# A fused attention and Mish block on one core: a new issue order, new buffers, and the first FFN's bias loaded in rows

## The chip, the cores and the metric

The kernel runs on one core of one Trainium2 chip. The metric is the device time of one execution in microseconds (us). A core has five instruction engines, each with a queue that it works off strictly in order: PE (TensorE, matrix products; PEld is its weight load), DVE (VectorE), ACT (ScalarE), POOL (GpSimd) and SP (SyncE, which here issues DMAs). An instruction waits in its queue for semaphores that other engines or DMAs set, and everything behind it on that engine waits with it.

## The reference

The block normalises x (2048 tokens of 512 numbers), runs a linear attention and a Mish network over it, and gates the one with the other. In outline:

```python
xn = layernorm(x)                                   # S, D = 2048, 512
qkv = xn @ wqkv                                     # 32 heads of 16
phi(u) = concat(softmax(u @ w_phi), softmax(-(u @ w_phi)))      # of each head, for q and k
kv, z = phi_k^T v, sum(phi_k)
s = (phi_q kv / (phi_q z + 1e-6)) @ wo
h = xn @ w1 + b1                                    # F = 1792
g = silu((h * tanh(softplus(h))) @ w2)
out = x + s * g
```

All is float32.

## The kernel before

The tokens lie in 16 tiles of 128 on the partitions. Every operand of a product is split into a part hi and a rest lo, and one product of float32 is three passes of TensorE (`mm3`: lo x hi, hi x lo, hi x hi). ACT writes hi, DVE or POOL writes lo = source - hi.

At the start, the weights of k and q are multiplied by `w_phi` on TensorE: `folded` makes one fold (`wkf`, `wqf`), and `wkh`, `wkl`, `wqh`, `wql` are its two parts. There are four folds for k and four for q. Meanwhile `norm(t)` loads a tile of x; takes its statistics (DVE alone for tiles 0, 1, 4 and 5; for the others ACT, in two passes into a scratch tile `dev`, with sums in `st` and `mv`); POOL takes the power -1/2 (`rs`); DVE makes `nb`; one instruction scales x in place; TensorE transposes it into a PSUM bank (`pt`), and `xT` receives the two parts of the transpose. Tiles go in pairs t and t + 4: `sums_x` copies the second transpose (`xr`) and makes four sums and differences of the two (`ts`), so that pairs of tiles and pairs of weight blocks need seven products where eight would do otherwise (the weights' sums are `ws`). Tiles 0 and 4 are also multiplied in the plain way (`k_0`, `v_0`, `v_4`). Results of k go through two softmaxes (`k0m` is the maximum and minimum of each head, `k0e` the differences to them), and `zacc` adds them up. q is written to DRAM and read again later. Then come the attention sums, the first FFN in the same seven-product manner (`fx`, `fz`, `fy`), the second FFN with the Mish at its load (`load_m`, which adds the bias `b1t`), and the output tile by tile (`final`): Silu, times s, plus x, store.

No engine's order is left to a scheduler. The parts are built in the order of a table `ORDER`, but building only records: every operation is put into a list by the class `Program`. Where an operation may run on either of two engines (`either`: DVE or POOL; `copy`: DVE or ACT; the scaling of x likewise), both forms are recorded. At the end, `issue()` goes through the text table `SCHED`: a number is an operation, and a letter behind it (V, G, A for DVE, POOL, ACT) picks an engine other than the first recorded. The order of `SCHED` is thus the order of every engine's queue at once, and since all instructions are issued by one line, they all show as L184 in the profile. All DMAs are issued by SP, except the first in the list, which goes to ACT's queue; eight hardware lanes take them in turn (`DMAHW0` to `DMAHW7`).

The second table, `PLACE`, gives the buffer of each tile in the order in which tiles are asked for: a bank of PSUM (eight), a slot of 4 KB (`slot`), a slot of 2 KB (`s2`), and so on. Two tiles with the same buffer are ordered by semaphores: the later one's first write waits for the last read of the earlier one.

The first 11 products of `wake`, on a tile of ones, use nothing that is loaded, and stand ahead of the folds.

In the rows of the issue order, names carry the number of the tile's allocation. `x_152`, `pt_158`, `xT_156` belong to tile 0; `x_180`, `pt_186`, `xT_184` to tile 1; `x_164`, `pt_170`, `xT_168`, `xr_171`, `ts_172` to tile 4; `x_216`, `pt_222`, `xT_220` to tile 5; `x_227`, `x_252`, `x_241`, `x_280`, `x_371` to others. `wkf_162` and `wkf_161` are folds of the first half of k's weights, `wkf_179` and `wkf_178` of the second; `v_215` is the value product of tile 0, `v_273` of tile 4, `q_238` and `q_279` the q of tiles 0 and 1, `q_207` and `q_250` of tiles 4 and 5.

Of the kernel before, what the change touches and what calls it, by code (L numbers as in the profile page):

```python
# [50 lines left out]
179V 410 158 237 189 411 62 286 61G 141V 180 238V 241 226 319 239 242 243 137 244 197 124 117 287 217 445 245 142 246
190V 583 412 185 181 63 338 288 321 320 247 82 107 167 123V 143 168 165A 198 218 182 267 219 339 199V 303 340 186A
248V 144V 169A 341 170 249 413 108V 200 253A 125 289V 250 109G 201 254 255V 204A 227 257 446 202 322 203 233 396 145
323 251 324 621 110 331V 256G 373 229 183 187 205 216 325 230 207V 414 447 90 397 220 268G 415 342 206V 262 234V 399
398 208 228A 449 146 290 263 161 450 111 451 294A 162G 315 221A 112 448 304V 332 222 305 264A 316V 343 416A 91 265
333G 166 126A 364 252 297V 223 306 258 235 295 224 374 260 259G 296V 344 269 231A 400 298 375 317 291 365A 307 271 377
401 326V 299 378 270V 417 379 354 376 309G 272 402 380 381V 327 273 382 355 275G 334 386A 292 403A 274 113G 293 350
261 387 452 622V 418 345A 351 388V 335A 300V 328 366 352A 624V 356 346 367A 358G 336 421V 383 301 347 308 623G 209 440
384 276G 422 211 390 368 277 481 353 357 453A 389V 359G 430 348 92 310G 360 329 479 431 330 210G 311 159 432 467 480A
419 441A 482 454 468A 278 212 404 391 434G 369 433 405 483 458A 435G 370 423V 279 424G 436 406 442 93G 425 437 469 393  # L60
443V 371A 625G 349 426 494 232 470 302 361 427G 496 495A 506 497 392G 455 472 491 438 407 507 225 439G 492A 461V 312
372 394 531 508A 484 459 509 529 460G 498 511G 527 530V 485G 471 544 313 280G 510 462 541 499 545A 500G 456 532 543
542A 486G 533 362 512G 547 528A 501V 734 444 585V 385 502 473V 428 548V 487 474G 573 493 513 363V 546 463 488 517 464G
549 534 554 514 584G 673 561 518 555A 429 314V 420 613 535G 580 562 599 489 536G 556 586G 571 614V 537 515 519 516G
595 538 640 563 521G 663 520 667 564 582 465 581V 594 707 574A 490V 575 572A 475 565V 659 596 587V 566G 735 503 633
522G 597A 678 476 592G 603 567 477 523 568 557 634A 478G 664 569 558 604 539 524 570G 550 665 605 643 593V 600 671
615V 598 657 616V 588 504 551 658A 661 525 674V 505V 636 660 526V 559A 637 618V 617 716G 635 676V 620 641A 737G 619V
638A 632 601A 717G 626 662 682 466 606 666 560 675G 576 683A 577 669 589V 630V 647 578A 552A 579 709 553 700 631V 679V
668 644 672 627V 457 602 729 607V 720 639 540V 701A 685 590 608V 591V 645A 642 646 686V 670 721G 687 628 708 648 702
718G 649 684 677G 724 703V 651V 690 719V 730A 722 629V 704 609 710V 749 705 711G 610 706 742 723G 846 750A 691 650 731  # L70
743A 680 652G 745 732 725A 692 681G 653 726 611 746A 688 736 689 744 1017 772V 738G 733 851 761 693 727 612G 778 739
751 654 844 800 712 694V 752 747 695G 765 655 748 656V 696 758 848 876 766V 845 697 755 698 768 740 699G 754 773V 774
762V 775G 777 759 852 769A 843 779 788 1059 763 808 753V 855 776G 819V 820 789 713 877 767 854 786G 790V 764 791 793
821 770 787G 796 802 771 853 814 871 797 714 824 865 756A 825V 894 794A 822 801 823 872V 826 830 811 757 780 827A 803G
856 1061 728 828 804G 792 889 929 829A 781V 878 782G 868 741 835V 857G 783 873 850 805 798 784 795 907 866A 812 836
813 891 899G 964 867 869 849 884 890V 858 942 885A 900 908A 859G 837G 926 943A 860 918V 895A 981 892 785 879V 886 982A
1067 838 919 870 880G 893 955 815G 839 881 847 806 910 816G 1025 927V 901G 840G 807 951 817 920V 902 921 874 809A 818G
903 944 887 952A 882 930G 888 1008 909 932G 861 1019 933G 958 862V 841V 863G 957 831 883 953 938 922 954 842 799 931G
1110 896 923V 1109 904G 939A 1068 905G 983 945 897 864 928 999 934 984 906 956A 935G 961 940 1111 810 911 1028 898
1010G 924V 941 913G 1013 977 1018 1029 948 978A 925 1030 936 1014G 832 972 760 962 1009V 946A 985 1011V 1020V 1115  # L80
973A 875 949 1021G 1038 979 991V 1022 974 959A 1122 1012V 1004 937V 960 1040 947 986A 1005G 992 1015 987 988 833 1039A
980 966 950 993V 1031 1000V 963 1041 1002G 989 1001G 1054 912 1032A 1026A 1016V 1108 1042 1033 1117 914V 994 1069 915
1056 1003V 965 1006 1152 1034 1296 1055V 1144 995 1007G 975 1051 1035A 1123 976 1119 1057 1130 916 1058 996G 1070V
1114 1079 1124 1071G 997V 1186 1121 1080A 1052A 1081 998 1043V 1125G 1082 1036 1075 1060 917 1023 1053 1076A 967G
1083A 1084 1163 968G 1024 1145 1062G 1166 1044 1063G 1086 1100V 1116 1118 1064 1133 1131A 1101 1155G 1164A 1132 1072
834 1138 1065 990 1187A 1037 1077 1085 1169 1092G 1113 1298 1146 1136 1170A 1156 1089 1066 1137A 1102V 969 1139 1198
1093 1140 1087A 1270 1112 1103 970 1141 1120 1207 1147G 1157V 1191 1045G 1090 1148G 1046 1171 1192A 1047 1158 1048V
1126V 1049G 1188 1297 1127 1104 1159 971 1194 1199V 1105G 1160G 1073 1212 1161G 1195A 1153 1388 1172 1143 1134 1173
1149 1106G 1361 1189 1078 1142A 1050 1200 1242 1272 1190 1167 1165 1178G 1193 1824 1107 1201 1074 1088 1196 1154G 1150
1197 1204 1213V 1174 1162 1279G 1208 1210 1205 1247 1202A 1214 1219 1334G 1374 1175A 1280 1216 1506 1362 1151 1128  # L90
# [839 lines left out]
```

## Time and profile before

| what | before |
|---|---|
| device time, median of 3 runs | 489.47 us (489.24 to 489.83) |
| the profiled execution, its span | 488.0 us |
| busy, PE | 481.5 us (99%) |
| busy, DVE | 429.3 us (88%) |
| busy, ACT | 284.6 us (58%) |
| busy, POOL | 244.5 us (50%) |
| data moved | 115.55 MB, 237 GB/s |

Busy time is that of instructions that compute: waiting and issuing don't count. The profiled execution is one run of the same program with its own time, a little under the median of the others. In rows of single instructions the first number is the start in us from the span's start, the second the length; `out<-in` names the tiles with their numbers left out; a bracket at the end tells how long the engine stood idle before, and whose end released it. TensorE's products overlap a little, and a row of several lists the start of the first and the time from there to the end of the last.

### The profile page before, as it was taken

How to read it: one execution, taken by the hardware profiler on the slowest of the kernel's cores; microseconds unless marked ns; L12 is line 12 of the kernel's file. 1: busy time of each engine (PE TensorE's matmuls, PEld its weight loads, DVE VectorE, ACT ScalarE, POOL GpSimd, SP SyncE). 2: the span in 40 equal slices, each digit the busy share in tenths (PEclk: the TensorE clock that was granted, in tenths of full speed). 3: DMA queues.
4: the chain of work that ended last, by engine and by line, in shares of the span. 5: the costliest groups of instructions: out<-in, count | busy, mean ns of one | idle time of the engine just before them, and what ended most of it. 6: DMA issues, size and time to landing. Idle time of an engine off the chain costs nothing.

```text
span 488.0 us, 8581 instructions
## 1 busy us (share of the span) xinstructions
PE 481.5 (99%) x3122; PEld 397.9 (82%) x3122; DVE 429.3 (88%) x687; ACT 284.6 (58%) x447; POOL 244.5 (50%) x188
## 2 busy tenths in 40 slices
PE   9999999999999999999999999999999999999995
PEld 9888888888888888888888878888888887888884
DVE  5989898899999997999999989998678588879984
ACT  5998777235154504325434676598976677576721
POOL 2675859967335786686557963312622032412021
PEclk9999999999999999999999999999999999999999
DMA  8956649165686789879969979788486615468543
GB/s 303 346 169 233 245 173 365 69 192 198 207 289 223 234 294 303 303 213 357 333 214 283 363 242 332 239 274 279 167 262 217 230 56 163 152 210 284 168 147 140
DMA packets 65594, 115.55 MB, mean 237 GB/s; under 512 B 7056, under 2 KB 32016, under 8 KB 65552
## 3 DMA queue, kind: packets, MB, share of 16 engines
q1 hardware_dynamic: 65408, 114.98, 69.9%
q8 instruction: 24, 0.39, 0.3%
q14 instruction: 18, 0.15, 0.1%
q10 hardware_dynamic: 144, 0.03, 0.0%
HBM read 72.92 MB, written 42.07 MB: 236 GB/s over the span
## 4 chain that ended last, share of the span: by engine, by line
PE 99%; DVE 0%; ACT 0%; DVEq 0%; issue 0%; ACTq 0%
PE y L184 20%; PE fx L184 16%; PE q L184 9%; PE pw L184 9%; PE kx L184 8%; PE x L184 8%; PE fy L184 8%; PE ky L184 4%; PE fz L184 4%; PE pn L184 2%; PE kz L184 2%; PE z L184 2%; PE kvp L184 2%; PE pt L184 1%; PE v L184 1%; PE k L184 1%
## 5 line engine op out<-in xcount | busy, mean ns | idle before, releaser
L184 PE MATMUL q<-wqh,xT 128*128 128x512 f32 x128 | 42.3, 393 | 0.0
L184 ACT ACTIVATE r<-r,b1t 128x512 f32<-128x512 f32 x56 | 38.1, 719 | 1.2 <-DMA r<-hd 1.1
L184 PEld LDWEIGHTS q<-wqh,xT 128*128 128x128 f32 x128 | 24.0, 188 | 5.0
L184 PE MATMUL q<-wql,xT 128*128 128x512 f32 x64 | 24.9, 390 | 0.0
L184 ACT ACTIVATE hc<-fx 128x512 f32<-128x512 f32 x11 | 6.5, 599 | 26.8 <-PE fx L184 15.9
L184 ACT ACT_TABLE_LOAD x16 | 20.5, 1283 | 0.3
L184 POOL TENSOR_TENSOR rs<-rs,mhalf 128x1 f32<-128x1 f32 x16 | 9.7, 615 | 19.7 <-DVE rs L184 19.7
L184 DVE TENSOR_REDUCE tz<-ez 128x64 f32<-128x1024 f32 x16 | 19.2, 1206 | 0.1
L184 PE MATMUL kx<-wss,th 128*128 128x512 f32 x56 | 17.3, 390 | 0.0
L184 POOL TENSOR_TENSOR tl<-ts,th 128x1024 fp32r<-128x1024 f32 x6 | 14.4, 2407 | 4.5 <-ACT th L184 3.1
L184 DVE TENSOR_TENSOR ol<-pn,oh 128x256 fp32r<-128x256 f32 x32 | 11.9, 416 | 5.1 <-ACT oh L184 5.1
L184 POOL TENSOR_TENSOR w1al<-w1a,w1ah 128x768 fp32r<-128x768 f32 x4 | 8.2, 2046 | 14.2 <-DVE w1sl L184 9.2
L184 POOL TENSOR_TENSOR w<-w2r,w 128x512 fp32r<-128x512 f32 x7 | 9.9, 1428 | 9.3 <-ACT w L184 9.3
L184 ACT ACTIVATE qs<-q 128x512 f32<-128x512 f32 x15 | 8.7, 594 | 9.4 <-PE q L184 5.0
L184 PEld LDWEIGHTS q<-wql,xT 128*128 128x128 f32 x64 | 12.0, 188 | 2.4
L184 ACT ACTIVATE oh<-pn 128x256 fp32r<-128x256 f32 x32 | 10.7, 393 | 4.9 <-PE pn L184 3.6
L184 POOL TENSOR_TENSOR w1s<-w1a 128x256 f32<-128x256 f32 x9 | 8.9, 995 | 7.4 <-PE q L184 7.1
L184 PE MATMUL pw<-oh,wo0l 128*128 128x512 f32 x32 | 12.4, 389 | 0.0
L184 PE MATMUL pw<-ol,wo0h 128*128 128x512 f32 x32 | 12.4, 389 | 0.0
L184 PE MATMUL pw<-oh,wo0h 128*128 128x512 f32 x32 | 12.4, 389 | 0.0
L184 PE MATMUL pw<-oh,wo1l 128*128 128x512 f32 x32 | 12.4, 389 | 0.0
L184 PE MATMUL pw<-ol,wo1h 128*128 128x512 f32 x32 | 12.4, 389 | 0.0
(869 smaller groups left out, 1833.1 us busy)
## 6 DMA issues: line engine op xcount, KB each, us to landing
r<-hd SPq DMA_DIRECT2D x28, 512.0 KB, 5.0
x<-x SPq DMA_DIRECT2D x16, 256.0 KB, 6.1
scr<-xT SPq DMA_DIRECT2D x8, 512.0 KB, 5.1
scrT<-th SPq DMA_DIRECT2D x8, 512.0 KB, 3.5
qd<-qs SPq DMA_DIRECT2D x16, 256.0 KB, 4.6
scrT<-tl SPq DMA_DIRECT2D x8, 512.0 KB, 4.8
qp<-qd SPq DMA_DIRECT2D x16, 256.0 KB, 5.1
xx<-xt SPq DMA_DIRECT2D x16, 256.0 KB, 4.9
```

The costliest lines, as they stand in the source:

```text
L184: getattr(g, m)(*a, **k)
```

## The change

Two things are edited. The first is the bias of the first FFN, 1792 numbers, which is held as `b1t` with 128 partitions and 14 columns. Before, the array lies in DRAM as it comes, and the load picks for each partition 14 numbers that are 128 apart. After, the array is laid out as 128 rows of 14 before the launch, and the load takes rows.

The second is the pair of tables. The operations are the same, numbered alike; `SCHED` has a new order and for many operations another engine, and `PLACE` has other buffers.

```diff
-        Q.dma_start(b1t, b1.rearrange("(c p) -> p c", p=P))
+        Q.dma_start(b1t, b1)
...
-        "b1": np.ascontiguousarray(B_b1),
+        "b1": np.ascontiguousarray(np.asarray(B_b1).reshape(FC, P).T),
...
 SCHED = """
-11 25 0 13 1 14 2 44 3 72 4 12 17 5 94 6 26 16 7 15 27 8 28 127 29 9 10 18 36 30 31A 45 95 40 37 46 147 47 73 32 41 19
+0 1 2 3 4 5 6 25 11 7 8 9 10 12 94 96 26 27 28 29 30 16 68 31V 14 72 97 73 74 75 40 43V 98 32 41 71A 69 18 13 22 36 17
...
```

Over the whole program the list of DVE goes from 689 rows to 654, that of ACT from 424 to 408, that of POOL from 193 to 241; a row is one instruction, or several alike in a row. The list of PE has 2078 rows where it had 2076, and that of SP 322 in both.

The following rows are from the start of the program. First PE, before: from the transposes of another tile (`pt_248`) through the value products of tiles 4 and 0.

```order
L184 MATMUL pt_248<-ident,x_241 128x128 [waits DVE_49]
L184 MATMUL pt_248<-ident,x_241 128x128 x3
L184 MATMUL v_273<-wv0h,xT_168 128x512 [waits DVE_49,PE_49]
L184 MATMUL v_273<-wv0l,xT_168 128x512 [waits Pool_49]
L184 MATMUL v_273<-wv0h,xT_168 128x512 x2
L184 MATMUL v_273<-wv0l,xT_168 128x512
L184 MATMUL v_273<-wv0h,xT_168 128x512
L184 MATMUL v_215<-wv0h,xT_156 128x512 [waits DVE_49]
L184 MATMUL v_215<-wv0l,xT_156 128x512
```

PE after: the end of the q of tile 0, and the value product of tile 0.

```order
L184 MATMUL q_238<-wqh_148,xT_156 128x512 x2
L184 MATMUL q_238<-wql_149,xT_156 128x512
L184 MATMUL q_238<-wqh_148,xT_156 128x512
L184 MATMUL v_215<-wv0h,xT_156 128x512 [waits DVE_49,PE_49,Activation_49]
L184 MATMUL v_215<-wv0l,xT_156 128x512
L184 MATMUL v_215<-wv0h,xT_156 128x512 x2
L184 MATMUL v_215<-wv0l,xT_156 128x512
L184 MATMUL v_215<-wv0h,xT_156 128x512
L184 MATMUL q_207<-wqh_195,xT_168 128x512 [waits DVE_49]
```

`v_215` has moved ahead, from row 92 of PE's list to row 67. Its bank is now the one that held `pt_170`, the transpose of tile 4.

Next DVE, before: the rows around the parts of tile 4's transpose.

```order
L184 TENSOR_TENSOR wql_149<-wqf_150,wqh_148 128x512
L184 TENSOR_TENSOR ts_172<-xr_171,pt_158 128x256 [waits Activation_49]
L184 TENSOR_TENSOR xT_184<-pt_186,xT_184 128x512 [waits Activation_49]
L184 TENSOR_TENSOR xT_168<-pt_170,xT_168 128x512 [waits Activation_49]
L184 TENSOR_SCALAR nb_221<-mv_217,rs_219 128x1 [waits Pool_49]
L184 TENSOR_TENSOR wql_196<-wqf_198,wqh_195 128x512 [waits Activation_49]
L184 TENSOR_TENSOR ts_172<-pt_170,xr_171 128x256
```

DVE after: the stretch up to the last read of `pt_170`.

```order
L184 TENSOR_TENSOR ws_294<-wkr_159,wvr_208 128x1024 [waits DMAHW0_49]
L184 TENSOR_SCALAR mv_228<-st_229 128x1
L184 COPY kp_188<-k_187 128x512 [waits DMAHW1_49,PE_49]
L184 COPY xr_171<-pt_170 128x512 [waits Activation_49]
L184 TENSOR_REDUCE k0m<-kp_188 128x32 [waits DVE_49]
L184 TENSOR_SCALAR st_282<-st_282 128x1
L184 TENSOR_TENSOR ts_172<-pt_170,xr_171 128x256 [waits DVE_49]
L184 TENSOR_TENSOR k0e<-kp_188,k0m 128x32x16 [waits DVE_49]
L184 TENSOR_TENSOR wv0l<-wvr_208,wv0h 128x1024
L184 TENSOR_TENSOR ts_172<-xr_171,pt_158 128x256
L184 TENSOR_TENSOR ts_172<-pt_170,ts_172 128x256 [waits DVE_49]
L184 TENSOR_TENSOR xT_168<-pt_170,xT_168 128x512
```

`xT_168` goes from row 31 of DVE's list to row 48, and `xr_171`, `wv0l` and `ws_294`, which were ACT's and POOL's, are DVE's now and stand ahead of it.

Last, ACT and POOL after, at the same place. ACT from the scaling of tile 4 to the hi part of its transpose:

```order
L184 ACTIVATE x_164<-x_164,nb_169,rs_167 128x512 [waits DMAHW5_49,DVE_49]
L184 ACTIVATE wkr_175<-wkf_178 128x512
L184 ACTIVATE dev_255,st_254<-x_252 128x512 [waits DMAHW1_49]
L184 ACTIVATE dev_244,st_243<-x_241 128x512 [waits DMAHW4_49]
L184 ACTIVATE wv0h<-wvr_208 128x1024 [waits DMAHW0_49]
L184 ACTIVATE xT_168<-pt_170 128x512 [waits PE_49]
```

Before, `x_164` was scaled by DVE, in its row 20, and `xT_168<-pt_170` was row 19 of ACT's list; it is row 25 now. POOL's list, the change as it stands between before (-) and after (+):

```order
 L184 TENSOR_TENSOR rs_155<-rs_155,mhalf 128x1
 L184 TENSOR_TENSOR rs_183<-rs_183,mhalf 128x1
+L184 TENSOR_TENSOR rs_219<-rs_219,mhalf 128x1
 L184 TENSOR_TENSOR rs_167<-rs_167,mhalf 128x1
-L184 TENSOR_TENSOR rs_219<-rs_219,mhalf 128x1
-L184 TENSOR_TENSOR ts_172<-xr_171,ts_172 128x256
+L184 TENSOR_TENSOR rs_231<-rs_231,mhalf 128x1
 L184 TENSOR_TENSOR ws_235<-wvr_208,wvr_211 128x1024
-L184 TENSOR_TENSOR rs_231<-rs_231,mhalf 128x1
-L184 TENSOR_TENSOR wv0l<-wvr_208,wv0h 128x1024
-L184 TENSOR_TENSOR k0e<-kp_188,k0m 128x32x16
+L184 TENSOR_TENSOR ws_251<-ws_235,wkr_159 128x1024
```

`rs_167` is tile 4's power. `wv0l` and one half of `k0e` have left POOL, `ws_251` and behind it `wv1l` have come forward. On SP, tile 4's load goes from the 4th place to the 13th, and a half of q's weights that stood further back stands ahead of it.

More of the change, by code (lines that the diff above doesn't have):

```diff
@@ L51 @@
[L51 to L90, printed above, removed]
@@ new lines @@
+309G 261 354 269 364 292 225 146 61G 509 344 381A 446 299 327 355 112 345A 346 357 400 300V 328 347 348 365V 382 383
+270A 417 418 421A 335A 448 447 419 422 210G 386V 449 423V 353 293 481 479 480V 450 442 366 425 336 203 260 252 212 424G
+359V 443A 401 402 403A 367A 387 529 368 384 585G 451 356 452 453A 329 430 431 482 358V 63 623G 511G 513 54 385 302 330
+93G 389G 388G 311 483 440 271 272 390 273 432 274 275V 276G 530V 541 531 532 301 391 393 349 426 514 515 433 454 404
+491 542A 428 232 427G 455 405 360 458A 459 441A 469 369 492A 527 528A 444 361 362 406 456 435V 460G 625V 484 370 534
@@ new lines @@
+461G 113G 371V 434V 462 493 392G 486G 485G 516G 496 586G 372 533 535G 536G 467 547 548A 494 495A 463 468A 664 457 429
+211 464G 466 663 661 543 544 571 517 497 498 363V 470 580 549 499 581V 500G 501G 561 518 520 592G 593G 436 545A 562 557
+554 546 599 626 555A 600 519 472 312 587V 564 437 313 314G 438 471 502 573 574A 487 613 566V 615V 439G 616G 277 278
+473G 488 556 633 582 594 617 522V 420 407 465 627G 474G 558 603 604 489 606 563 640 559A 634V 503 662 588 589G 641A
+601A 572A 614A 642 682 683A 715 717G 671 279 605 684 280V 490V 636 575 635 637 700 521G 523 690 657 550 647 659 394 668
@@ new lines @@
+859V 912 1001G 905G 1060 837V 911 906 1025 938 1008 895A 939A 1026A 928 942 883 914V 966 874 807 1063G 1062G 945 860
+838 913V 940 861 943A 1064 756A 951 955 847 760 870 941 799 893 948 918V 952A 915 1100V 862G 949 909 958 839 1009V 946V
+1010G 956V 1101 950 1017 875 1109 1011G 1012G 840G 1013 1015 1014G 841G 863G 957 944 983 1028 977 978A 1004 1065 953
+919 1003G 1018 1067 929 934 897 1108 898 954 979 864 959V 1069 961 985 1029 930V 1027 1112 1038 988 1019 916 989 1030
+984 1117 1005G 1040 1169 935G 932G 933G 931G 1054 962 1020V 1039V 986V 842 972 1006 936 1055A 973V 1041 757 974 1056
@@ new lines @@
+1261 1231 1267 1255 1263 1317 1391 1444 1298 1257 1280 1179 1497 1278 1276 1277 1399 1293 1281G 1282 976 1283 1294V
+1223 1312 1429 1414 1379 1264 1265 1381 1398 1431 1362 1268 1313V 1295 1314 1374 1177 1334V 1363V 1297 1128 1299V 1129
+1094G 1269 1284G 1285G 1180G 1095 1181 1182 1183G 1151 1096 1275 1323 1353 1366 1498 1380 1400 1324V 1556 1382 1243
+1245 1316 1392V 1430 1546 1203 1627 1365V 1287 1206 1547 1417 1367A 1288A 1350 1286 1244V 1097V 1548 815G 1184G 816G
+1383G 1445 1078 1197 1165 1519 1481 1432 1499 1246G 1386 1290 1289 1395 1384 1319V 1335 1336G 1337 1482 1338 1385 1375
@@ new lines @@
+1500 1415 1376V 1185 1433G 1387 1396 1483 1401V 1513 1521 1377 1378G 1339V 1405 1394 1404 1393 1402 1098G 1418G 1300G
+1501G 1505 1452 1438 1325 1514 1454 1351A 1446 1099 1291V 1318V 1504 1437 1403 1436 1520 1439 1447V 1440G 1301 1354A
+1522 1304V 1305 1168 1302 1303 1306V 1307 1523G 1502 1416V 1434 1435 1449 1340G 1341 1453 1455 1549 1456V 1462 1550V
+817 1342 1343 1308 1524 1503 1526 1345V 1441 1442G 1448 1320 1326V 1467 1570 1572 1424 1355 1533 1215 1468 1309V 1344
+1327 818V 1427 1425 1469 1485V 1346G 1561 1563 1562 1310V 1428G 1527 1451 1450 1525 1564 1633 1352 1591 1368 1555 1474
@@ new lines @@
+1705 1601 1610 1602 1617 1618 1656 1596 1599 1597 1598 1512 1511 1538 1539 1528 1419 1603 1604V 1685 1612 1607 1608
+1657 1658 1659V 1588V 1465G 1687G 1688G 1420V 1421G 1613V 1660V 1662G 1605 1706 1635 1619 1589 1590 1606 1614 1358V
+1690V 1691 1663 1545 1091 1615 1629 1620V 1529G 1636V 1637V 1664V 1628 1765 1791 1466 1621 1697 1725 1359 1751 1746
+1422 1622 1639 1360G 1707V 1640 1625V 1623V 1666 1624 1423V 1626 1692V 1650 1648 1646 1644 1647 1642 1643 1630V 1698G
+1530G 1665 1693 1694 1654 1531 1652 1649 1651 1653 1645 1655 1641 1770 1732 1689G 1726G 1747V 1532G 1766V 1667 1369
@@ new lines @@
+1713 1670 1671 1668 1682 1674 1678 1672 1676 1727 1728 1683 1669 1679 1675 1767G 1661V 1771G 1768 1680 1792V 1748V
+1769G 1708G 1677 1681 1579 1780 1752 1733 1762 1834 1753 1714V 1673 1631V 1754G 1772G 1773 1715V 1370V 1774V 1801 1695
+1701 1702A 1781 1734 1755V 1580V 1735V 1757V 1581V 1699V 1783V 1736V 1738V 1371V 1723G 1793G 1756V 1782 1794 1795G 1749
+1835A 1763V 1710 1784V 1582 1743 1716 1868 1802 1583V 1816 1869V 1717V 1700 1703 1638 1632 1836 1837 1737V 1804V 1817V
+1750G 1803 1739 1740V 1372 1373V 1729 1883 1742 1805G 1830 1758 1759V 1841 1787 1788V 1711V 1518 1775 1818 1796 1819
@@ new lines @@
+1741 1760 1789 1808 1886 1809V 1761 1810 1831V 1842V 1838V 1806G 1786G 1807G 1812V 1776G 1887G 1873 1730A 1921 1731
+1712 1845 1814A 1790 1811 1916 1889 1865 1815A 1849 1826 1917G 1866G 1777G 1785G 1853 1813V 1820V 1850V 1821V 1877
+1878V 1846V 1797G 1798G 1833 1840 1844 1832 1839 1884V 1843 1847 1764 1709 1744A 1778 1779G 1880 1871 1745 1872 1824
+1899 1905 1881G 1892 1857 1822 1799 1800G 1854V 1874G 1858V 1823V 1875G 1848 1851 1890G 1852 1855 1859 1885 1825 1827V
+1863 1904 1856 1937 1860 1828G 1861 1862 1900 1906 1894 1901V 1864 1867 1907G 1908V 1912 1911 1876 1893 1898 1895V
@@ L125 @@
+1896V 1913V 1922 1910 1936 1919 1920 1931 1932 1933 1934 1902G 1935 1897 1909 1914V 1915 1950 1938 1939G 1940G 1941
+1951G 1942 1943G 1944V 1952V 1903 1953 1946 1947V 1948V 1949 1945 1829 1870 1879 1882 1888 1891 1918 1923 1927 1924V
+1928V 1925V 1926 1929V 1930
 """
 PLACE = """
[20 rows of a table removed]
[20 rows of a table added]
 """
```

73 lines of the change are left out of this document (35 added, 38 removed), and 40 rows, old and new, of the table PLACE.

## The prediction
> **What bounds the kernel now.** I read the page's shares first, then the busy time by stretch. In the rows by stretch the columns are the stretch, its length, the busy time of PE, PEld, DVE, ACT and POOL with their instructions, the granted clock, the DMA share and GB/s.
>
> ```profile
> span 488.0 us, 8581 instructions
> PE 481.5 (99%) x3122; PEld 397.9 (82%) x3122; DVE 429.3 (88%) x687; ACT 284.6 (58%) x447; POOL 244.5 (50%) x188
> PE 99%; DVE 0%; ACT 0%; DVEq 0%; issue 0%; ACTq 0%
> ...
> 1.10:6.00 4.90, 4.89 (x23) 4.89 (x24) 1.63 (x4) 1.28 (x2) 1.17 (x5) 1.00 0.85 277
> 6.00:20.00 14.00, 14.00 (x102) 12.98 (x102) 12.59 (x34) 12.40 (x25) 5.31 (x7) 1.00 1.04 385
> 20.00:60.00 40.00, 39.92 (x192) 32.82 (x191) 35.44 (x96) 36.13 (x75) 29.34 (x23) 1.00 0.63 227
> 60.00:280.00 220.00, 220.00 (x1457) 182.33 (x1456) 209.06 (x303) 94.64 (x135) 150.41 (x105) 1.00 0.76 255
> 280.00:480.00 200.00, 200.00 (x1345) 162.95 (x1344) 167.59 (x242) 139.21 (x210) 57.83 (x45) 1.00 0.65 214
> 482.80:487.20 4.40, 0.00 (x0) 0.00 (x0) 1.43 (x4) 0.66 (x2) 0.00 (x0) 1.00 0.23 76
> 487.20:488.00 0.80, 0.00 (x0) 0.00 (x0) 0.00 (x0) 0.00 (x0) 0.00 (x0) 0.55 0.00 0
> ```
>
> The chain that ends last is 99% TensorE, and the stretches show why: from 6 us to the last product TensorE lacks 0.08 us of work in all. What is not TensorE is 1.1 us ahead of the first warm-up product and 5.2 us behind the last product (488.0 less 482.8). So a new order of the same products can win next to nothing, while every wait that it brings to TensorE is paid in full. The question is therefore only whether TensorE waits anywhere in the new list. The time is told against this execution, whose span of 488.0 lies 1.5 us under the median of 489.47; I add what changes to the median.
>
> **Where the new list is thinnest.** TensorE's own work up to the first value product `v_215` is counted with these rows (start, length, what):
>
> ```profile
> 1.11 5.04 PE wake L184 x22
> ...
> 6.15 1.78 PE wkf L184 x16
> 7.94 0.44 PE pt L184 x4
> 17.38 1.36 PE kz L184 x6
> ```
>
> A fold of one weight tile is half of 1.78, 0.89 us; a tile's four transposes 0.44; six products 1.36. The warm-up keeps its 11 products, so the folds start where they do now, at about 6.0 us. The new list puts ahead of `v_215` eight folds, four transposes and 48 products (k, kz, kx and the q of tiles 1 and 0): 6.0 + 8 x 0.89 + 4 x 0.44 + 8 x 1.36 = 25.8 us. Now `v_215` uses the bank in which `pt_170` stood, the transpose of tile 4, and so it waits until DVE has read that bank for the last time, in `xT_168`, row 48 of DVE's list. Tile 4 is the very one that was pushed back: its load goes from SP's 4th place to the 13th, and its `x_164` behind the statistics of other tiles. I follow that chain with what one instruction after another takes in this trace (start, length).
>
> ```profile
> 7.97 0.60 ACT L184 ACTIVATE wkh<-wkf 128x512 fp32r<-128x512 f32 x1 [0.30 <-PE wkf L184]
> ...
> 19.73 1.07 ACT L184 ACTIVATE wv0h<-wvr 128x1024 fp32r<-128x1024 f32 x1
> 20.68 0.64 ACT L184 ACTIVATE dev<-x 128x512 f32<-128x512 f32 x1
> ...
> 21.30 0.63 ACT L184 ACTIVATE dev<-x 128x512 f32<-128x512 f32 x1
> ...
> 22.61 0.60 ACT L184 ACTIVATE xT<-pt 128x512 fp32r<-128x512 f32 x1
> 23.09 0.73 ACT L184 ACTIVATE dev<-x,st 128x512 f32<-128x512 f32 x1
> ...
> 23.80 0.82 ACT L184 ACTIVATE x<-x,nb,rs 128x512 f32<-128x512 f32 x1
> 24.50 0.63 ACT L184 ACTIVATE dev<-x 128x512 f32<-128x512 f32 x1
> ```
>
> ```profile
> 19.80 1.22 DVE L184 TENSOR_TENSOR ws<-ws,wkr 128x1024 f32<-128x1024 f32 x1
> 20.93 0.21 DVE L184 TENSOR_SCALAR nb<-mv,rs 128x1 f32<-128x1 f32 x1
> ...
> 23.48 0.68 DVE L184 TENSOR_REDUCE k0m<-kp 128x32 f32<-128x512 f32 x1
> 24.08 0.68 DVE L184 TENSOR_TENSOR xT<-pt,xT 128x512 fp32r<-128x512 f32 x1
> 24.68 0.42 DVE L184 TENSOR_TENSOR ts<-pt,ts 128x256 f32<-128x256 f32 x1
> ```
>
> From start to start: ACT needs 0.95 for 1024 columns, 0.62 for a `dev`, 0.48 for an eviction, 0.70 for an `x`; DVE 1.13 for 1024 columns, 0.60 for 512, and about 0.33 for 256 (0.42 less the overlap of 0.08 that the other rows have).
>
> First to tile 4's scale. The sixth fold, `wkf_162`, is done at 6.0 + 6 x 0.89 less one fold plus one transpose: 6.0 + 5 x 0.89 + 0.44 = 10.9. ACT takes it 0.2 later and needs three evictions before DVE's `wkl_161` is let go: 11.1 + 0.96 + 0.60 = 12.7. From there DVE has eight instructions of 512 columns (4.8) and six small ones (0.5): 18.0. Its next, the scaling of `x_216`, meets POOL's power for tile 4, and with it `nb_169` is ready at 19.1. (Tile 4's load is not what is late: it is the 14th piece of 256 KB; 4.9 us at 277 GB/s bring five of them by 6.0, and at 385 GB/s the nine others need 6.1 more, 12.1.)
>
> Then ACT: `x_164` at 19.2, and TensorE can transpose it at 20.0, 0.2 later than it would have. Behind `x_164` ACT has an eviction, two `dev` and `wv0h` before it reads the transpose: 19.2 + 0.70 + 0.48 + 2 x 0.62 + 0.95 = 22.6, done at 23.2. DVE's `xr_171` waits for that, and then come `xr_171` (0.60), `k0m` (0.60), a small one, `ts` (0.33): `k0e` arrives at 24.8. Then `k0e` 0.60, `wv0l` 1.13, two `ts` of which one waits for the other (0.75) and `xT_168` (0.68): 28.0. TensorE wants `v_215` at 26.0 (25.8 and the 0.2), so without anything else it waits 2.0 us, and no other product stands ready, since its queue is in order.
>
> **The shared port.** There is something else: `k0e` and `wv0l` read two operands from SBUF, and POOL has three instructions of 1024 columns in a row at this place (`ws_235`, `ws_251`, `wv1l`).
>
> ```profile
> 16.56 2.41 POOL L184 TENSOR_TENSOR ws<-wvr,wvr 128x1024 f32<-128x1024 f32 x1
> 18.93 0.55 POOL L184 TENSOR_TENSOR rs<-rs,mhalf 128x1 f32<-128x1 f32 x1
> ...
> 113.95 1.22 DVE L184 TENSOR_TENSOR zacc<-k0e,k4e 128x1024 f32<-128x1024 f32 x1
> ...
> 171.80 1.94 POOL L184 TENSOR_TENSOR k15e<-k15e,k15r 128x1024 f32<-128x1024 f32 x1 [3.85 <-DVE k15r L184]
> 172.65 2.16 DVE L184 TENSOR_TENSOR zacc<-zacc,k13e 128x1024 f32<-128x1024 f32 x1
> ...
> 116.21 1.55 DVE L184 TENSOR_TENSOR k12e<-kp,k12m 128x512 f32<-128x512 f32 x1
> 117.18 1.51 POOL L184 TENSOR_TENSOR k7e<-k7m,kp 128x512 f32<-128x512 f32 x1
> 117.69 1.28 DVE L184 TENSOR_TENSOR w1s<-w1a,w1s 128x256 f32<-128x256 f32 x1
> ```
>
> An addition of `zacc` alone takes 1.22; the one at 172.65 took 2.16, and ended 1.07 after POOL's instruction did (174.81 against 173.74): the two exclude each other for a whole instruction. The last three rows show who is next when both have work: they take turns, each waiting for the one that came before it. In the new list POOL's `rs_231` comes while DVE has `ws_294` (19.9 to 21.0) and ends at 21.5; `ws_235` ends at 23.9, `ws_251` at 26.3. `k0e`, which arrived at 24.8, runs from 26.3 to 26.9; `wv1l` has waited since 26.3 and runs to 29.3; `wv0l` ends at 30.4, `xT_168` at 31.9. TensorE waits 31.9 - 26.0 = 5.9 us. I take this end, because the rows show the port held so, and keep 2.0 as the other.
>
> **The rest of the change.** The bias is loaded as 14 neighbouring numbers a row, where it was single numbers.
>
> ```profile
> L184 ACT ACTIVATE r<-r,b1t x56: 704/712/772, 274.1 to 437.0; 128x512 f32<-128x512 f32 x56
> L184 SPq DMA_DIRECT2D b1t<-b x1: 427/427/427, 214.2 to 214.2; - x1
> ```
>
> Issued at 214.2 and first used at 274.1, it costs nothing before and after; it keeps its place in SP's list within four rows. If SP issued it 50 us later it would still be covered. Between 60 and 480 us the new list gives DVE 35 rows fewer (654 for 689) and POOL 48 more (241 for 193). DVE is busy for 209.06 of 220 us now and TensorE still never waits; with fewer rows its margin grows, so this part I cost at nothing. What covers it is POOL, which has 150.41 of 220 now; if that cover goes, a late POOL instruction of 1024 columns costs its 2.4 us once. At the end, the last Silu, two multiplications, two additions and two stores stand as they stood, so the tail of 5.2 us stays. The sum: 489.47 + 0.2 + 5.9 = 495.6.
>
> **The rivals.** A shorter wait: if `k0e` comes 0.9 us earlier than I have it, it passes ahead of `ws_251`, `wv0l` follows `ws_251` at 26.9, and `xT_168` ends at 29.5; with no meeting at the port it ends at 28.0. That gives 3.5 and 2.0 us, 491.7 to 493.2. For it speaks that my terms are rounded over a dozen steps; against it, that each step is bounded by a row. Chance 0.17.
>
> The clock drops in the wait. The last product ends at 482.7 and the clock column reads 1.00 up to 487.2 and 0.55 for the last 0.80, so it fell some 4.5 us after the work ended. A wait of 5.9 us is longer than that. Coming back, the chip took from 1.11 to about 6.0 with warm-up passes of 0.23 us (5.04 by 22) where the folds' passes take 0.11: half the work of 4.9 us is lost, 2.45, and the time is 498.0. Against it: one fall is all that the trace shows, and my wait needs to be only 1.4 us too long to be under it. Chance 0.20. The Trainium skill, page "TensorE: Matmul & The Clock Gate", section "HAM oscillation — how this bites in real kernels", says that TensorE is throttled again after idle gaps of more than about 3.4 us, and its section on the clock gate that this window runs free; by that rule a gap of 5.9 us holds a whole window in (5.9 - 3.4) / 3.4 = 0.7 of its positions, an estimate from the page, and one of 2.0 us never. The fall 4.5 us after the last product agrees with it.
>
> No wait at all: the chain has slack that I don't see, or the read of the bank comes earlier than DVE's list makes it. Then the time is that of before, 489.0 to 489.9. For it speaks that DVE is as full now (35.44 of 40 us, ACT 36.13) with 0.08 us lost; against it, that I must be off by 2 us even with the port left out. Chance 0.23.
>
> Faster: TensorE's work is full, so a gain must come from the 5.2 us behind the last product. Its two stores would have to land a full 1.0 us sooner, and nothing moved ahead of them does that: one more store of 256 KB now stands just in front of them in SP's list. It decides from 0.98 us on. Time 488.0 to 488.5, chance 0.05. A late POOL elsewhere, 492, has what is left, 0.03.
>
> **How the numbers follow.** The case that I forecast, the wait behind the port at full clock, has 0.32, and its own range is 493.8 to 496.8. A measurement of this kernel tells 0.2%, 0.98 us, from no change: slower is 0.32 + 0.17 + 0.20 + 0.03 = 0.72, the same 0.23, faster 0.05. The range goes from 489.0, which takes in the case of no wait, to 497.5, which leaves out the faster case and the greater part of the clock's.
>
> **What would show it.** In the profile after: one gap of TensorE at 26 us, ended by DVE `xT`, and TensorE's busy time still near 481.5. DVE's `xr` ending ACT's `xT` wait near 23; `k0e` and `wv0l` much longer than 0.68 and 1.22 beside three POOL instructions of 2.4. A clock column under 1.00 between 30 and 37 us would show the clock's case. If TensorE has no gap before 60 us, the walk is wrong; if the gap is there but ended by ACT or a load, its cause is another.

## The result, and the profile after

The changed kernel takes 519.64 us (519.42 to 521.57, four runs) where the kernel before took 489.65 us beside it (489.24 to 489.93, four runs): a ratio of 1.0623, with a 95% interval from 1.0604 to 1.0642. It is 30 us slower. The forecast was 495.6, with a range up to 497.5.

The page of the profiled execution, first lines: its span, and the busy time of each engine with its share and its instructions.

```profile
span 517.7 us, 8542 instructions
PE 493.4 (95%) x3122; PEld 399.9 (77%) x3122; DVE 450.6 (87%) x654; ACT 273.9 (53%) x431; POOL 340.9 (66%) x236
```

The span has grown by 29.7 us. TensorE's idle time is 517.7 - 493.4 = 24.3 us where it was 6.5, so 17.8 of them are waits; its busy time is 11.9 longer for the same 3122 instructions. (Of the 11.9, some 4.0 are slow clock, as told below. Another 6.6 lie within half a us of the twenty waits of 0.02 us or more: products in a row start every 0.23 us and overlap, each is drawn 0.39 us long, and at a wait the overlap is lost. So a wait costs about 0.3 us more than its gap shows.) And DVE, which has 33 instructions fewer, is busy for 21.3 us more.

The busy time by stretch, in the columns of the prediction (stretch, length, PE, PEld, DVE, ACT, POOL with their instructions, granted clock, DMA share, GB/s); the last product ends at 512.3.

```profile
6.00:20.00 14.00, 13.84 (x99) 12.65 (x99) 11.75 (x30) 9.90 (x23) 2.29 (x4) 1.00 1.04 400
20.00:60.00 40.00, 34.78 (x152) 27.99 (x151) 33.01 (x79) 27.26 (x56) 26.62 (x21) 0.91 0.30 113
60.00:280.00 220.00, 215.20 (x1433) 176.69 (x1432) 202.87 (x295) 94.83 (x139) 164.98 (x110) 1.00 0.73 247
280.00:512.30 232.30, 224.64 (x1420) 177.71 (x1418) 199.43 (x242) 139.70 (x211) 145.31 (x94) 0.99 0.63 211
512.30:517.70 5.40, 0.03 (x1) 0.00 (x0) 1.47 (x5) 0.66 (x2) 0.00 (x0) 0.97 0.52 169
```

Between 20 and 60 us TensorE lacks 5.2 us, between 60 and 280 it lacks 4.8, and from there to the last product 7.7. The tail is 5.4 us, as it was. The waits of TensorE, by the tile that it waited to produce and the instruction whose end released it, in us in total, times and longest:

```profile
PE v L184 <- DVE st L184: 5.1, 1, 5.1
PE pw L184 <- DVE ol L184: 2.5, 2, 2.1
PE kvp L184 <- issue: 2.4, 2, 1.2
PE fx L184 <- DVE w1al L184: 2.2, 1, 2.2
PE y L184 <- DVE h L184: 1.6, 1, 1.6
...
PE y L184 <- DVE a12l L184: 0.8, 1, 0.8
PE z L184 <- DVE ma9l L184: 0.7, 1, 0.7
PE pn L184 <- DVE ol L184: 0.7, 1, 0.7
PE y L184 <- DVE mb12l L184: 0.6, 1, 0.6
```

The first row is the wait that was forecast: `v_215`, at 26.11. (The small `st` named there ran at that moment; the semaphore that came with it was that of `xT`, which ended at 31.09.) The others in the list are released by DVE too, but for the two pauses in `kvp`: "issue" means that the trace shows nothing that TensorE waited for there. What holds DVE up at 26 us is in the rows of single instructions (start, length, engine, tiles): first POOL's, then DVE's.

```profile
20.98 2.41 POOL L184 TENSOR_TENSOR ws<-wvr,wvr 128x1024 f32<-128x1024 f32 x1
23.47 2.41 POOL L184 TENSOR_TENSOR ws<-ws,wkr 128x1024 f32<-128x1024 f32 x1
25.82 2.80 POOL L184 TENSOR_TENSOR wv1l<-wvr,wv1h 128x1024 fp32r<-128x1024 f32 x1
```

```profile
22.77 0.69 DVE L184 COPY xr<-pt 128x512 f32<-128x512 f32 x1 [1.51 <-ACT xT L184]
...
24.36 2.06 DVE L184 TENSOR_TENSOR k0e<-kp,k0m 128x512 f32<-128x512 f32 x1
26.34 3.35 DVE L184 TENSOR_TENSOR wv0l<-wvr,wv0h 128x1024 fp32r<-128x1024 f32 x1
...
30.41 0.68 DVE L184 TENSOR_TENSOR xT<-pt,xT 128x512 fp32r<-128x512 f32 x1
```

`k0e` waits for `ws_251` to end, `wv1l` waits for `k0e`, and `wv0l` waits for `wv1l`: turn by turn, as the prediction walked it. The same picture stands at 161 us, where the forecast had nothing: first POOL, then DVE, then TensorE.

```profile
160.40 5.55 POOL L184 TENSOR_TENSOR w1sl<-w1s,w1sh 128x1024 fp32r<-128x1024 f32 x2 [0.49 <-PE q L184]
```

```profile
160.57 3.13 DVE L184 TENSOR_TENSOR w1al<-w1a,w1ah 128x768 fp32r<-128x768 f32 x1
```

```profile
163.85 0.47 PE L184 MATMUL fx<-fb0h,w1al 128*128 128x512 f32 x1 [2.23 <-DVE w1al L184]
```

POOL's first `w1sl` started 0.17 us before DVE's `w1al`, which then took 3.13 us and not the 0.95 that `w1al` takes in the kernel before, and TensorE stood for 2.23. To have one number for this, I took for each operation and shape of DVE the 5th percentile of its lengths as what it takes alone, and added up what all its instructions take beyond that: 40 us in the kernel before, 91 us after. This is a rough measure, since instructions of one shape differ for other reasons too.

The clock fell behind the first wait, and behind one at 446 us. Windows over the changed kernel, same columns:

```profile
26.00:29.00 3.00, 0.11 (x1) 0.00 (x0) 3.00 (x2) 0.13 (x1) 2.62 (x1) 1.00 0.00 0
29.00:30.00 1.00, 0.00 (x0) 0.00 (x0) 1.00 (x2) 0.00 (x0) 0.00 (x0) 0.66 0.00 0
30.00:36.00 6.00, 4.77 (x11) 3.80 (x12) 5.16 (x19) 3.82 (x10) 2.17 (x3) 0.50 0.00 0
...
450.00:452.00 2.00, 2.00 (x6) 1.60 (x5) 2.00 (x5) 0.00 (x0) 0.61 (x1) 0.50 0.04 8
```

At 0.50 a pass starts every 0.43 us and not every 0.23; twelve such passes until 36.1 cost 2.4 us. The second slow stretch, 3.4 us from 449.2 on, costs half its length, 1.7.

### The profile page after: what moved, and what is told of

Read it like the earlier page. It is cut to its first block, busy times and chain, and to the rows that moved or that the text cites. A ratio compares the mean times of both kernels' runs of the same rounds, so it can differ in the third digit from the quotient of the medians.

```text
span 517.7 us, 8542 instructions
## 1 busy us (share of the span) xinstructions
PE 493.4 (95%) x3122; PEld 399.9 (77%) x3122; DVE 450.6 (87%) x654; ACT 273.9 (53%) x431; POOL 340.9 (66%) x236
## 5 line engine op out<-in xcount | busy, mean ns | idle before, releaser
L184 PE MATMUL q<-wqh,xT 128*128 128x512 f32 x128 | 43.6, 399 | 0.1
L184 POOL TENSOR_TENSOR rs<-rs,mhalf 128x1 f32<-128x1 f32 x16 | 12.5, 791 | 26.9 <-DVE rs L184 26.9
L184 ACT ACTIVATE hb<-fx 128x512 f32<-128x512 f32 x9 | 5.4, 599 | 30.1 <-PE fx L184 17.5
L184 POOL TENSOR_TENSOR w<-w2r,w 128x512 fp32r<-128x512 f32 x7 | 11.6, 1662 | 10.2 <-ACT w L184 6.8
L184 POOL TENSOR_TENSOR w1sl<-w1s,w1sh 128x1024 fp32r<-128x1024 f32 x6 | 15.9, 2671 | 0.6 <-PE q L184 0.5
L184 POOL TENSOR_TENSOR tl<-ts,th 128x1024 fp32r<-128x1024 f32 x6 | 15.9, 2644 | 0.1
L184 PE MATMUL pn<-ph,kvw 32*32 32x256 f32 x512 | 13.3, 385 | 1.1 <-DVE ol L184 0.7
L184 ACT ACTIVATE w<-w2r 128x512 fp32r<-128x512 f32 x14 | 8.4, 623 | 10.8 <-PE pw L184 5.1
L184 DVE TENSOR_TENSOR xT<-pt,xT 128x512 fp32r<-128x512 f32 x16 | 10.8, 680 | 3.7 <-ACT xT L184 3.1
L184 DVE TENSOR_TENSOR ha<-ha,fz 128x512 f32<-128x512 f32 x14 | 9.4, 668 | 4.9 <-PE fz L184 2.9
```

Source lines behind the costliest of these rows:

```text
L184: getattr(g, m)(*a, **k)
```

## The experiments

The theory was that DVE's instructions with two operands in SBUF and POOL's exclude each other and take turns, everywhere and not only at 26 us, and that DVE's lateness is what TensorE pays. The rival was that the new order itself (what stands behind what, and late landings) does it, whichever engine works and however long.

**The bias alone** (`e1_bias`), in the kernel before:

```diff
-        Q.dma_start(b1t, b1.rearrange("(c p) -> p c", p=P))
+        Q.dma_start(b1t, b1)
```

> The kernel before, with the new layout and load of the bias alone; both tables stay. Theory of the port (the loss of 30 us is made by the new lists, above all by vector instructions of DVE and POOL that take turns on a shared port): 489.65 us, within 0.5 either way, since the bias is loaded once and long before its use. Rival (the loads' landings are disturbed by the bias's scattered read, and the row layout moves them): off by more than 1 us, either way.

Measured: 489.86 us against 489.92, ratio 0.9998 (0.9989 to 1.0007). The bias is no part of it; the 30 us come from the tables.

**Engines and order, crossed** (`e2_old_engines`, `e3_new_engines`). In the first, the changed table's order with the old letters behind 60 us (215 operations, the first pair of lines); in the second, the old order with the new letters (239 operations, the second pair).

```diff
-508V 343 60 416V 159 258 291 315 235 259V 316A 294A 265 137 170 183 62
+508A 343 60 416A 159 258 291 315 235 259G 316V 294A 265 137 170 183 62
...
-128 118 65 67V 78A 70 51 148 171 22 129 66 55A 213 149 130 281
+128 118 65 67A 78V 70 51 148 171 22 129 66 55V 213 149 130 281
```

> The changed kernel, where every operation issued behind 60 us runs on the engine that it had before; order and buffers stay as changed. Theory of the port (what is lost behind 60 us comes from the vector work given to POOL): only the wait at 26 us (5.1 us) and the slow clock behind it (2.3 us) remain, so 497 to 500 us, with the sum of what DVE's instructions take beyond their shortest back from 91 us to under 55. Rival (the new order and the new buffers lose it, whichever engine works): 514 us or more, and TensorE's gaps behind 60 us are still there, 10 us or more in all.

> The kernel before, with its order, its buffers and its bias, where every operation runs on the engine that the changed table gives it. Theory of the port: 502 to 520 us, with gaps of TensorE ended by two-operand instructions of DVE that overlap one of POOL. Rival (order and buffers): under 494 us.

Measured: 558.26 us (ratio 1.1407, 1.1388 to 1.1426) and 536.52 us (1.0959, 1.0944 to 1.0975). Both are slower than either kernel, so the first expectation of the theory fell: old engines in the new order don't give back what is lost behind 60 us, they lose 39 us more. What I had named as the rival's sign in that run, 514 us or more with over 10 us of gaps behind 60 us, came true. DVE's sum beyond its shortest lengths is 74 us in the first and 98 in the second. The second lies beyond the theory's range on the slow side, and is no proof of it, since the first shows that a mismatch of order and engines can be dear by itself. These two runs decide nothing between the theory and its rival, and the port had to be taken away in another way.

**DVE's list at 24 us in another order** (`e4_xt_first`):

```diff
-... 58V 88V 120V 56 57V 53 173 ...
+... 58V 56 57V 53 120V 88V 173 ...
```

(88 is `k0e`, 120 `wv0l`, 56 and 57 two of the sums `ts`, 53 the lo part `xT_168`.)

> The changed kernel, with five operations of DVE in another order at 24 us: the last reads of tile 4's transpose (two sums and the lo part) and then wv0l go ahead of the differences k0e. Theory of the port with turns: the bank is free at about 25.7, wv0l goes between POOL's second and third long instruction and ends at 27.1, TensorE's wait falls from 5.1 to about 1 us, the clock does not fall behind it, and the time is 519.6 - 4.1 - 2.3 = 513.2, or somewhat more (up to 516) where later waits take part of it back. Rival (tile 4's chain is late by itself, whatever the port does): a wait of 3 us or more stays and the time is 517 or more.

Measured: 518.16 us (1.0569, 1.0551 to 1.0588); the profiled execution has a span of 514.5, 3.2 less than after. DVE's rows there:

```profile
24.95 0.68 DVE L184 TENSOR_TENSOR xT<-pt,xT 128x512 fp32r<-128x512 f32 x1
25.55 1.22 DVE L184 TENSOR_TENSOR wv0l<-wvr,wv0h 128x1024 fp32r<-128x1024 f32 x1
26.68 2.87 DVE L184 TENSOR_TENSOR k0e<-kp,k0m 128x512 f32<-128x512 f32 x1
```

The walk held: `wv0l` slipped in ahead of `wv1l` and took 1.22 us, and the wait of `v_215` shrank to 0.57. But the turn was then paid by `k0e`, which waited for `wv1l`, and behind it TensorE waited 1.93 us for tile 5. So 2.5 us of waits were left where I expected 1, and the clock stayed up. The profiled execution, the fastest of the four, gained 3.2 us, the median only 1.5. So the mechanism went as the theory has it, but the time of 518.16 lies over its upper end of 516 and where I had put the rival.

**Only `k0e` and `wv0l` with one operand** (`e8_two_alone`). `i` is the operation's number:

```diff
+                if i in (88, 120) and e == "V" and m == "tensor_tensor" and single(a):
+                    b = a[1] if k["op"] != ALU.subtract or spread(a[2]) else a[2]
+                    g.tensor_reduce(a[0], one_more(b), axis=X, op=ALU.max)
+                    continue
                 getattr(g, m)(*a, **k)
```

> The changed kernel, where only the two instructions k0e and wv0l at 24 us are replaced by ones that read one operand (k0e is not reduced by the maximum, wv0l is a copy of the hi part). Theory of the port: k0e ends at 25.0, wv0l at 26.2, the bank is free at 28.0, TensorE's wait falls from 5.1 to 1.9 us, the clock stays up, and the time is 519.6 - 3.2 - 2.3 = 514.1, or up to 517 where later waits take part of it back. Rival (the wait at 26 us comes from tile 4's late chain alone): a wait of 4.5 us or more and 519 us.

Measured: 514.80 us (1.0512, 1.0496 to 1.0528). DVE's rows at the place:

```profile
24.34 0.67 DVE L209 TENSOR_REDUCE k0e<-kp 128x512 f32<-128x512 f32 x1
24.94 1.21 DVE L209 TENSOR_REDUCE wv0l<-wv0h 128x1024 fp32r<-128x1024 f32 x1
...
26.85 0.68 DVE L211 TENSOR_TENSOR xT<-pt,xT 128x512 fp32r<-128x512 f32 x1
```

Beside the same three instructions of POOL, the two take 0.67 and 1.21 us, TensorE's wait is 1.6 and not 5.1, and no slow clock follows it. Of the 5.1 us, then, 3.5 were turns at the port and 1.6 the late chain of tile 4.

**TensorE kept busy while it waits** (`e7_filler`):

```diff
                     mm3(ps, (xT[t][:, 0, k, :], xT[t][:, 1, k, :]), w[k], k == 0, k == KC - 1)
+                for _ in range(23 if t == 0 and i else 0):
+                    PE.matmul(ps, zeros_r, xT[t][:, 0].rearrange("p k n -> p (k n)"), start=False, stop=True, skip_group_check=True)
```

> The changed kernel, where TensorE does 23 products with a tile of zeros into the bank of q of tile 0 while it waits at 26 us (they add zero, 5.2 us). Theory (the clock falls because TensorE is idle, and costs twelve passes 0.2 us each): the clock column stays at 1.00 from 26 to 40 us and the time falls by 2.3 to 517.3 us, within 0.7. Rival (the clock falls for another cause, or later waits take the 2.3 us back): the clock falls all the same, or the time is 519 us or more.

Measured: 516.77 us (1.0557, 1.0539 to 1.0575), 2.9 less than the changed kernel. Its windows:

```profile
26.00:31.00 5.00, 5.00 (x23) 4.06 (x22) 4.97 (x5) 0.21 (x1) 2.76 (x1) 1.00 0.00 0
31.00:36.00 5.00, 5.00 (x23) 3.96 (x22) 4.19 (x16) 3.68 (x10) 2.02 (x3) 1.00 0.00 0
```

With TensorE busy, the clock stays at 1.00 through both. Idleness it is at this place, and the gain of 2.9 us bears out the price of 2.4 roughly: behind it the two pauses in `kvp` are 2.2 us shorter and two new waits of 1.5 us in all have come. (The wait at 161 us, 2.26 us here, was now followed by slow passes, where in the changed kernel it was the one at 446 us.)

**DVE with one operand throughout** (`e5_one_operand`, and `e6_before_one_operand` as its control): the same lines without the condition on `i`, and

```diff
-        A.activation(e, e, AF.Exp)
+        A.activation(e, e, AF.Exp, scale=0.001)
```

> The changed kernel with its order, engines and buffers, where each addition and subtraction of DVE with both operands in SBUF and 256 columns or more is replaced by a reduction over an axis of one element, which has the same number of columns but reads one operand; the second operand's part of the computation is left out, and the exponentials' arguments are scaled by 0.001 so that they stay finite. Theory of the port (such instructions and POOL's take turns, and DVE comes late by that): DVE's instructions get back to their shortest lengths (busy 450 us to about 400), nearly all gaps of TensorE go except 2 us at 26 us, and the time is 490 to 497 us. Rival (the order and the engines put too much on DVE, or late landings do it, whatever the port): over 510 us.

> The kernel before with the same replacement, as a control. Both theories: 489.6 us, within 0.7, since TensorE is busy throughout already; more would mean that the replacement itself costs time.

Measured: 498.42 us (1.0176, 1.0161 to 1.0191), and the control 489.53 us (0.9993, 0.9983 to 1.0002). Span and engines of the first:

```profile
span 496.8 us, 8524 instructions
PE 485.2 (98%) x3122; PEld 398.2 (80%) x3122; DVE 393.6 (79%) x654; ACT 273.3 (55%) x431; POOL 295.8 (60%) x236
```

Order, engines and buffers are those of the changed kernel; only the second operand is gone, and the exponentials' arguments are scaled. DVE is busy for 57 us less and POOL for 45 us less, though POOL does all that it did. DVE's sum beyond its shortest is 34 us and not 91, and POOL's, taken the same way, 18 and not 63. (The control has 25 on DVE, so what is left of the sum is mostly no waiting at the port.) The time falls by 21.2 of the 30 us. What is left of waits:

```profile
PE kvp L211 <- issue: 2.3, 2, 1.3
PE v L211 <- DVE st L211: 1.6, 1, 1.6
...
PE pw L211 <- DVE ol L211: 0.4, 1, 0.4
PE pn L211 <- DVE hb L211: 0.4, 1, 0.4
```

The time is 1.4 us over the range that I gave. The replaced instructions also drop a wait here and there (for the maxima above all), so a little of the 21.2 may be that. In the next pair the slower kernel does all of the block's work as it was; the other one is built on the control and shares this weakness.

**More work for POOL in the kernel before** (`e10_more_pool`), and the same in the control with one operand (`e11_more_pool_one`):

```diff
+        for n, s in enumerate(SCHED.split()):
+            if 270 <= n < 1870 and n % 20 == 0:
+                self.more()
...
+    some = ones[:, None, :].to_broadcast([P, 4, P])
+    prog.more = lambda: nc.gpsimd.tensor_tensor(extra, some, some, op=ALU.add)
```

> The kernel before, with 80 more instructions on POOL between 60 and 480 us that nobody waits for (512 columns of ones added to ones, some 1.3 us each, 104 us in all, about what the changed tables give POOL). Theory of the port: DVE's instructions with two SBUF operands take turns with them, DVE's sum beyond the shortest lengths goes from 40 to 70 us or more, and the time to 493 to 512 us. Rival (DVE's margin before is wide enough, and only the new order is narrow): 489.7 us, within 0.7.

> The same 80 instructions of POOL, in the control kernel (the one before, with DVE's additions and subtractions of 256 columns or more in SBUF replaced by reductions of one operand; exponentials scaled). Theory of the port: no more turns are taken, and only POOL's own results come later: under 491.5 us, at least half of what the 80 instructions cost in the kernel before is gone. Rival (it is POOL's lateness that costs): as slow as the kernel with the 80 instructions and DVE's two operands.

Measured: 518.86 us (1.0595, 1.0576 to 1.0615) and 492.23 us (1.0056, 1.0034 to 1.0077). First the engines of the one, then of the other:

```profile
PE 491.6 (95%) x3122; PEld 398.1 (77%) x3122; DVE 467.7 (91%) x687; ACT 284.8 (55%) x447; POOL 344.9 (67%) x268
```

```profile
PE 482.7 (98%) x3122; PEld 398.3 (81%) x3122; DVE 416.8 (85%) x687; ACT 284.3 (58%) x447; POOL 300.4 (61%) x268
```

The old order, the old engines, the old buffers: 80 additions that nobody reads bring POOL to 345 us, where the change brings it to 341, and cost 29.1 us (518.86 - 489.74), nearly what the change costs. DVE's sum beyond its shortest lengths rises from 40 to 79. Where DVE reads one operand, the same 80 cost 2.5 us over the kernel before (2.7 over the control's 489.53). In that kernel POOL's own lateness is thus worth under 3 us, and some 26 of the 29.1 go with the second operand: turns at the port, and one slow stretch of the clock that a wait of 2.1 us brought (3.4 us from 64.3 on, so 1.7). DVE has 17 us less to do in the control, so a part of POOL's lateness may be hidden there. The theory's sign was right and its upper end of 512 us too low; the control lies 0.7 over the 491.5 that I gave.

**The port by itself** (`e9_port_alone`), not the block but stages of like instructions:

> Not the block at all: stages that measure the port by itself (the output is filler). va: 12 additions-like products of DVE with two SBUF operands of 1024 columns, alone; gb: 8 of POOL alone; vc with gc: both at once; vd with gd: DVE has one operand in PSUM (512 columns, 20 times); ve with ge: DVE reduces one operand over an axis of one element; vf with gf: DVE scales one operand by a constant; vg with gg: DVE's two operands have 64 columns; vh with gh: POOL's instructions have 128 columns. Then TensorE runs blocks of 40 to 46 passes with waits of nine lengths between them. Theory of the port: va 1.13 us each from start to start, gb 2.4; vc and gc take turns one for one, so 8 pairs take 8 x (1.2 + 2.4) = 29 us; vd and ve are as long as alone; a small vg waits for a whole POOL instruction, about 2.4 us; rival (both slow each other a little at the same time): vc's instructions all grow alike, to 1.5 to 2.5, and gc's with them. Theory of the clock: it falls some 3 us after a wait began, so after waits of over 3.3 us always and under 1.5 us never.

Groups of instructions of its trace (count, then busy time and mean ns of one, then idle time before). First DVE's:

```profile
L81 DVE TENSOR_TENSOR vc<-a,b 128x1024 f32<-128x1024 f32 x12 | 28.8, 2402 | 0.4
L90 DVE TENSOR_SCALAR vf<-a 128x1024 f32<-128x1024 f32 x16 | 25.2, 1575 | 0.5
L81 DVE TENSOR_TENSOR vg<-a,b 128x64 f32<-128x64 f32 x12 | 17.7, 1476 | 0.4
...
L81 DVE TENSOR_TENSOR va<-a,b 128x1024 f32<-128x1024 f32 x12 | 14.7, 1225 | 0.4
L87 DVE TENSOR_REDUCE ve<-a 128x1024 f32<-128x1024 f32 x12 | 14.6, 1219 | 0.4
L84 DVE TENSOR_TENSOR vd<-a,pq 128x512 f32<-128x512 f32 x20 | 13.7, 686 | 0.7
```

POOL's, in the stages of the same letter:

```profile
L67 POOL TENSOR_TENSOR gc<-d,e 128x1024 f32<-128x1024 f32 x8 | 24.8, 3101 | 0.6
L67 POOL TENSOR_TENSOR gf<-d,e 128x1024 f32<-128x1024 f32 x8 | 21.1, 2634 | 0.5
L67 POOL TENSOR_TENSOR gd<-d,e 128x1024 f32<-128x1024 f32 x8 | 18.8, 2349 | 0.6
L67 POOL TENSOR_TENSOR ge<-d,e 128x1024 f32<-128x1024 f32 x8 | 18.8, 2348 | 0.5
...
L67 POOL TENSOR_TENSOR gb<-d,e 128x1024 f32<-128x1024 f32 x8 | 18.7, 2338 | 0.6
```

Alone, an instruction of 1024 columns takes 1.23 us on DVE (`va`) and 2.34 on POOL (`gb`). At once (`vc`, `gc`) they alternate: the median of `vc` is 3.24 us, its own time and most of POOL's, and the eight of `gc` take 24.8 us. A pair takes 3.28 us from start to start, a little less than the 3.6 that I expected, so the two overlap by some 0.3. With an operand in PSUM (`vd`) or a reduction (`ve`) neither notices the other. So the rival, in which both slow down a little, is out. The Trainium skill, page "SBUF — State Buffer", section "Who interferes with whom", says so too: the shared ports are an exclusive lock, a DVE instruction with two inputs in SBUF contends with a POOL instruction that reads SBUF, and reductions never contend on this chip. These rows agree, but for the small overlap. A stage with small instructions on POOL (`gh`, 128 columns) goes the same way: they take 0.45 us at their shortest and 1.31 in the median beside `vh`, which grows from 1.21 to 1.36.

## Why the prediction was wrong

The forecast ended at 495.6 and the time is 519.6. Its steps, one by one:

- *What bounds the kernel.* That every wait of TensorE is paid in full is borne out: 17.8 us of waits are in the span, and some 0.3 us around each of them come on top, which the forecast didn't have.
- *The wait at `v_215`.* Right in place, cause and nearly in size: forecast from 26.0 for 5.9 us, measured from 26.11 for 5.12, with `k0e`, `wv1l`, `wv0l` and `xT_168` in the order forecast, each a little earlier. The lower end, 2.0 without the port, measured 1.6.
- *The clock.* It was given 0.20 and a price of 2.45 us. It happened, and cost 2.4. The argument against it, that the fall comes some 4.5 us after work ends and my wait was hardly longer, was wrong: it came 3.2 us after TensorE went idle.
- *The bias* and *the tail*: nothing, as forecast.
- *The step that failed* is the sentence "with fewer rows its margin grows, so this part I cost at nothing", on DVE between 60 and 480 us, with its bound for a lost cover, a late POOL instruction's 2.4 us "once". I counted rows where I should have counted meetings. DVE's list became shorter by handing work to POOL, and each instruction that POOL gets holds the port against DVE's list, so what DVE was relieved of came back as waiting: 33 instructions fewer, 21.3 us more of busy time. Eighty idle additions on POOL price it: 29.1 / 80 = 0.36 us of the whole kernel for each (of 1.30 us in the mean with its own waiting, 1.04 without). The 48 further rows of POOL stood in my own text, and the rule of turns too, a paragraph above; I applied it to one place. "A late POOL elsewhere" had a chance of 0.03 and a time of 492.

So the 30 us are: at 26 us the wait of 5.1 and the slow clock of 2.4; behind that some 22. The whole share of the port, both places together and with the slow clock that its waits bring, is about 21.2 by the run without second operands; 3.5 and 2.4 of it belong to the wait at 26 us, so some 15 of the 22 are turns at the port elsewhere. The 8.8 left there are 1.6 of tile 4's late chain, 2.3 of two pauses within `kvp`, 0.8 before `pw` and `pn`, and 3.7 by which TensorE's busy time is over that of before, nearly all of it within half a us of the waits that are left.

What the two pauses in `kvp` are stays open: TensorE stands still among its 64-column products with no wait that the trace shows, in the changed kernel and in four others with its order, and not in those with the order before. The traces hold one lead that no run tests. In each of the five kernels a packet of 16 KB on the DMA queue that the profile calls `instruction` starts 1.2 to 1.6 us ahead of each pause; in the changed kernel it is at 124.2 and 179.3, and the pauses are at 125.7 and 180.5. With 23 products more ahead of them (the filler) such a packet comes just as the first stretch of `kvp` begins, and the pauses are down to 0.2 us. But in the kernel before one starts inside such a stretch, at 135.4, and no pause follows.

The sign to look for was named as "one gap of TensorE at 26 us". There are twelve gaps of 0.2 us or more in all, and most are ended by DVE.

## What to carry to other kernels

Moving work from a full DVE to an idle POOL isn't free even where nobody waits for POOL: with both operands in SBUF the two engines share a port, so count for each moved instruction how often DVE's two-operand instructions meet it. In a kernel whose DVE is 88% busy and whose TensorE never waits, that margin is the thing to protect; the share of busy time tells nothing of it, since time spent waiting for the port is shown as busy. An instruction that reads PSUM, or a reduction, passes freely, so give POOL its work where DVE has such ones. And an order of instructions found for one choice of engines need not be good for another: with the other's engines the two tables lost 39 and 47 us here.

## What was not expected of the hardware

A scaling by a constant, with a single operand in SBUF, takes turns with POOL as well: `vf` takes 0.68 us at its shortest and 2.71 each time that it meets one of POOL's instructions (the mean of 1.58 holds eight that ran when POOL was done), and POOL's `gf` grows from 2.34 to 2.63. And size doesn't matter to the wait: `vg`, of 64 columns, has a median of 2.35 us beside POOL, a whole POOL instruction, where its shortest is 0.21.

The clock falls after shorter waits than I thought. In the last part of the run on the port, TensorE ran blocks of 40 to 46 passes with waits between them; counting the passes that started more than 0.3 us apart at the start of the next block:

| wait, us | waits | followed by a slow clock |
|---|---|---|
| 0.58, 1.30 | 12 | 0 |
| 2.03 | 6 | 3 |
| 2.75 | 6 | 4 |
| 3.47 | 6 | 6 |
| 4.19 to 6.35 | 23 | 23 |

The clock column says the same in each of the 53 cases, and the expectation for this part held: always after more than 3.3 us, never after less than 1.5. Slow stretches are 7 to 14 passes, 1.4 to 2.8 us lost. The Trainium skill, page "TensorE: Matmul & The Clock Gate", section "HAM oscillation — how this bites in real kernels", gives gaps of more than about 3.4 us as the limit. Above it these rows agree, every time; below it they don't: 7 of 12 waits of 2.0 to 2.8 us were enough, as was the one of 2.1 us at 446 us in the changed kernel (the one of 2.2 at 161 us was not), and the measurement decides.
